# Two layers of linear attention and gated MLP on one core: a small weight on another queue, a narrower tile of ones, a new order

## The chip, the cores and the metric

The kernel runs on one core of a Trainium2 chip. Its engines are named as the profile names them: PE is TensorE (matrix products), PEld its weight loads, DVE is VectorE, ACT is ScalarE, POOL is GpSimd and SP is SyncE, which here only issues transfers. The metric is the device time of one execution in microseconds. The kernel before takes 387.3 us, the median of three timed runs (387.19, 387.3 and 387.8).

## The reference

The input x has 2048 rows of 512 numbers in bf16. Two equal layers follow each other, each of them an attention block and a gated block, with a layer norm ahead of both and a residual added behind both:

```
q, k, v = layernorm(x) @ wqkv                     # 32 heads of 16
phi(t)  = [softmax(t @ w_phi), softmax(-t @ w_phi)]   # 32 features a head
kv, z   = sum over rows of phi(k) v, of phi(k)
x += ((phi(q) @ kv) / (phi(q) @ z + 1e-6)) @ wo
y  = layernorm(x)
x += (relu(y @ W_gate) * (y @ W_up)) @ W_down     # 512 -> 1376 -> 512
```

The sum over all rows divides a layer: no query can be finished before the last key of the layer is in `kv`.

## The kernel before

The rows lie in 16 tiles of 128. They are worked in five slabs, called stages, of 2, 4, 4, 4 and 2 tiles (`SLABS`). A stage of an attention block takes the statistics of its tiles (L866, L891), applies the norm (L908 on ScalarE, L911 on VectorE or GpSimd), turns the tiles over into `yA` (by PE products with `ident`, L732, and an eviction, L839 or L842; or by a transposing transfer, L916), makes keys and values (products with `Wkp` and `wv`, L728, the helper of all full products), takes exponentials (L969), their sums (L975) and reciprocals, scales the values with them (L989) and adds the products of keys and values to `kvsum` (L1001, L1011). `queries` makes the query features (L1070). `attend` makes the divisors, spreads them over the features (`abT`, through PE at L1207 for stages 0 and 1, through memory at L1143 and L1147 for the others), scales the query features (`scale`, L1192, or L1222 and L1225), makes the numerators by packed products (L1159), and goes through `wo` to the residual. `glu` has the gate and up products, the ReLU (L1281), the product (L1283), the down product and the residual (L1229). The last 96 of the 1376 columns are worked apart (`rest`, `Wl`).

`w_phi` is not applied to each row. At the start it is folded into the weights: `BD` is a block diagonal made of `wphi` (L830), the weights `Wknat` are turned over by PE (L732) and evicted into `hT` (L839, L842), multiplied with `BD` and evicted into `Wkp`. For the queries the weights are turned over by transposing loads (L757) and folded in the same manner into `Wqp`.

Until data are there, PE multiplies a tile of ones with itself: eight products (`NWARM`, L807) and then fillers (`FILL`, L812: 14 with ones, 8 with `Wkp` as the right side). Their results are not used. The ones lie in a part of `yG` that is free at the start, and are also what `ident` and the masks are cut from on GpSimd (L816 to L820).

The order of the work is not that of the program text. Each operation is recorded with its engine, what it reads and writes, and an estimated duration; `schedule` then places the operations one by one, the one that can start first ahead of the others, and among equals the one with the lower turn number, from the list `TURNS`. `plan` works out the semaphores that each waits for. So each engine has one fixed list of instructions, and each instruction waits only for what it needs. The engine of an operation is its default, or the one that the table `ENG` names for it: `ld/` are loads, `ms/` memsets, `ap/` the applied norm, `yc/` and `ot/` evictions, `es/` and `em/` the scaling of the query features, `vh/` the scaled values, `rz/` reciprocals, `za/` the eviction of the divisors' sums. The first figure behind the name is the layer, the second the stage.

At the start SyncE's queue holds x tile 0, the blocks 1 and 3 of the key weights, x tiles 2 and 3, x tiles 4 to 7, `wv`, x tiles 8 to 11, then a transposing load of a query weight, and more. ScalarE's queue holds x tile 1, block 0 of the key weights, `wphi` and block 2, and ScalarE loads its table of functions behind them (L789).

Of the kernel before, what the change touches and what calls it, by code (L numbers as in the profile page):

```python
# [9 lines left out]
ALU = mybir.AluOpType  # L10
ACT = mybir.ActivationFunctionType
AX = mybir.AxisListType
P = 128
# [17 lines left out]
 'ap/a10/0': 'pool',  # L31
# [4 lines left out]
 'ap/a12/2': 'act',  # L36
# [13 lines left out]
 'ap/g12/0': 'act',  # L50
 'ap/g12/2': 'act',
 'ap/g12/3': 'act',
# [10 lines left out]
 'em/11/11': 'dve',  # L63
 'em/11/13': 'dve',
 'es/02/0': 'pool',
 'es/02/1': 'pool',
 'es/03/0': 'pool',
 'es/03/1': 'pool',
 'es/04/0': 'pool',
 'es/04/1': 'pool',  # L70
 'es/04/2': 'pool',
 'es/12/0': 'pool',
 'es/12/1': 'pool',
 'es/13/1': 'pool',
 'es/13/2': 'pool',
 'es/14/0': 'pool',
 'fck0': 'dve',
 'fck1': 'act',
 'fck3': 'act',
 'ftk1': 'act',  # L80
 'ld/x1': 'act',
 'ms/ZD 0': 'pool',
 'ms/ZO 0': 'pool',
 'ms/kvs 0 1': 'pool',
 'ms/kvs eps 0': 'pool',
 'ot/00/0': 'dve',
 'ot/00/1': 'act',
 'ot/00/2': 'dve',
 'ot/01/3': 'dve',
 'ot/02/1': 'dve',  # L90
 'ot/02/2': 'dve',
 'ot/02/3': 'dve',
 'ot/03/2': 'dve',
 'ot/03/3': 'dve',
# [6 lines left out]
 'ot/11/1': 'dve',  # L101
 'ot/12/0': 'dve',
 'ot/12/2': 'dve',
# [3 lines left out]
 'ot/13/3': 'dve',  # L107
 'ot/14/1': 'dve',
 'ot/14/3': 'dve',
# [9 lines left out]
 'rz/1/0': 'act',  # L119
# [16 lines left out]
 'vc/1/4': 'dve',  # L136
 'vc/1/5': 'dve',
 'vc/1/6': 'dve',
 'vc/1/7': 'dve',
# [10 lines left out]
 'vh/0/9/1': 'dve',  # L150
 'vh/1/1/1': 'dve',
 'vh/1/11/0': 'dve',
 'vh/1/12/0': 'dve',
 'vh/1/13/1': 'dve',
# [3 lines left out]
 'vh/1/3/0': 'dve',  # L158
 'vh/1/4/0': 'dve',
 'vh/1/5/1': 'dve',  # L160
# [4 lines left out]
 'vh/1/9/1': 'dve',  # L165
# [34 lines left out]
 'za/02': 'dve',  # L200
 'za/12': 'dve',
# [425 lines left out]
def build_kernel(nc, A_x, A_wqkv, A_w_phi, A_wo, W_gate, W_up, W_down, out):  # L627
# [8 lines left out]
    with ExitStack() as ctx:  # L636
# [15 lines left out]
        yG = sb("yG", [2, NC, 512])  # L652
# [82 lines left out]
        def full(ps):  # L735
            return ps.f32()
# [675 lines left out]
```

## Time and profile before

| | |
|---|---|
| median of three timed runs | 387.3 us |
| the profiled execution as a whole | 386.95 us |
| its span, first to last instruction | 385.2 us |
| PE busy | 373.0 us (97%) |
| VectorE, ScalarE, GpSimd busy | 274.9, 194.0, 79.1 us |
| chain that ended last | PE 77%, VectorE 11%, ScalarE 5%, transfers 3% |
| moved by transfers | 27.44 MB |
| granted TensorE clock | 1.000 |

The profile is one execution. A row of its timeline gives the start, the time from the first start to the last end, engine, line of the kernel, operation, what is written from what is read, shapes and count; in brackets stands how long the engine was idle before it and what ended that. Products on PE overlap: a product of 512 columns is listed with some 380 ns, but the next one starts about 217 ns after it. A row of the table of stages gives for each engine its busy time in that stretch. A load's "us to landing" counts from its issue to its last semaphore update.

### The profile page before, as it was taken

How to read it: one execution, taken by the hardware profiler on the slowest of the kernel's cores; microseconds unless marked ns; L12 is line 12 of the kernel's file. 1: busy time of each engine (PE TensorE's matmuls, PEld its weight loads, DVE VectorE, ACT ScalarE, POOL GpSimd, SP SyncE). 2: the span in 40 equal slices, each digit the busy share in tenths (PEclk: the TensorE clock that was granted, in tenths of full speed). 3: DMA queues.
4: the chain of work that ended last, by engine and by line, in shares of the span. 5: the costliest groups of instructions: out<-in, count | busy, mean ns of one | idle time of the engine just before them, and what ended most of it. 6: DMA issues, size and time to landing. Idle time of an engine off the chain costs nothing.

```text
span 385.2 us, 8848 instructions
## 1 busy us (share of the span) xinstructions
PE 373.0 (97%) x3644; PEld 200.1 (52%) x3693; DVE 274.9 (71%) x559; ACT 194.0 (50%) x434; POOL 79.1 (21%) x68
## 2 busy tenths in 40 slices
PE   7999998999999999999999999989999999999996
PEld 4655454574445444454566455466544544445663
DVE  6999999878754795756299987678954666644333
ACT  4999999562430524255346579983262311413310
POOL 1087740030240521132023531004002110000000
PEclk9999999999999999999999999999999999999999
DMA  7997201142460222022002010214433121221011
GB/s 234 186 325 180 43 3 58 64 114 57 86 141 26 76 41 56 0 57 41 9 0 43 15 32 3 83 43 138 109 73 127 31 71 41 56 55 43 0 36 55
DMA packets 56969, 27.44 MB, mean 71 GB/s; under 512 B 39296, under 2 KB 55264, under 8 KB 56928
## 3 DMA queue, kind: packets, MB, share of 16 engines
q1 hardware_dynamic: 55824, 26.36, 27.6%
q10 hardware_dynamic: 1104, 0.51, 0.5%
q8 instruction: 29, 0.48, 0.5%
q14 instruction: 12, 0.10, 0.1%
HBM read 14.73 MB, written 4.00 MB: 49 GB/s over the span
## 4 chain that ended last, share of the span: by engine, by line
PE 77%; DVE 11%; ACT 5%; DMA 3%; issue 2%; SPq 2%; ACTq 0%
PE pb L728 72%; DVE stats L866 4%; PE pb L1001 2%; DMA wphi<-in_A_w_phi_dram 1%; DVE Zk L975 1%; ACT ytile L908 1%; DVE x_sb L1229 1%; SPq L916 1%; ACT expq L1070 1%; PE pb L1159 1%; DMA abT<-spread 1%; DMA yG<-ytile 1%; DVE ytile L911 1%; ACT gate_sb L1281 1%; SPq L1147 1%
## 5 line engine op out<-in xcount | busy, mean ns | idle before, releaser
L728 PE MATMUL pb<-yG,Wu 128*128 128x512 bf16 (+1 forms) x394 | 95.5, 336 | 1.1 <-DVE abT L839 0.3
L728 PE MATMUL pb<-Wd,hT 128*128 128x512 bf16 (+3 forms) x350 | 95.9, 372 | 0.5 <-issue 0.2
L728 PE MATMUL pb<-yG,Wg 128*128 128x512 bf16 (+1 forms) x394 | 93.3, 336 | 0.2
L1281 ACT ACTIVATE gate_sb<-pb 128x512 bf16<-128x512 f32 x80 | 46.9, 595 | 85.2 <-PE pb L728 63.9
L1283 DVE TENSOR_TENSOR hT<-gate_sb,pb 128x512 bf16<-128x512 bf16 x80 | 54.0, 682 | 49.7 <-PE pb L728 30.5
L1229 DVE TENSOR_TENSOR x_sb<-x_sb,pb 128x512 bf16<-128x512 bf16 x59 | 39.4, 679 | 26.2 <-PE pb L728 26.2
L728 PEld LDWEIGHTS pb<-yG,Wu 128*128 128x128 bf16 x400 | 38.9, 98 | 32.6 <-DVE abT L839 0.8
L728 PEld LDWEIGHTS pb<-yG,Wg 128*128 128x128 bf16 x400 | 38.8, 98 | 31.5 <-issue 0.6
L728 PEld LDWEIGHTS pb<-Wd,hT 128*128 128x128 bf16 (+1 forms) x363 | 34.8, 98 | 35.5 <-issue 1.1
L989 POOL TENSOR_TENSOR vhat<-vsb,rZk 128x544 bf16<-128x544 bf16 x29 | 31.9, 1118 | 79.7 <-ACT rZk L982 30.1
L1192 POOL TENSOR_TENSOR expq<-expq,abT 128x1024 bf16<-128x1024 bf16 (+1 forms) x12 | 21.5, 1799 | 123.5 <-DVE expq L1192 46.9
L866 DVE BATCH_NORM_STATS2 stats<-x_sb 128x6 f32<-128x512 bf16 x60 | 40.1, 683 | 0.3
L728 PE MATMUL pb<-wv,yA 128*128 128x512 bf16 x123 | 36.8, 379 | 0.5 <-issue 0.3
L728 PE MATMUL pb<-Wkp,yA 128*128 128x512 bf16 x123 | 35.7, 379 | 0.3 <-DVE yA L839 0.2
L1070 ACT ACTIVATE expq<-pb 128x512 bf16<-128x512 f32 x64 | 34.5, 621 | 1.2 <-PE pb L728 0.8
L728 PE MATMUL pb<-yA,Wqp 128*128 128x512 bf16 (+1 forms) x152 | 34.0, 335 | 1.1 <-issue 0.8
L728 PE MATMUL pb<-wo_sb,oT 128*128 128x512 bf16 x123 | 33.4, 379 | 0.2 <-ACT oT L842 0.2
L975 DVE TENSOR_REDUCE Zk<-expk 128x64 f32<-128x1024 bf16 x20 | 24.0, 1207 | 2.6 <-ACT expk L969 2.5
L969 ACT ACTIVATE expk<-pb 128x512 bf16<-128x512 f32 x40 | 22.0, 611 | 4.1 <-PE pb L728 3.0
L1249 ACT ACTIVATE gate_sb<-pb 128x192 bf16<-128x192 f32 x16 | 5.3, 329 | 33.7 <-PE pb L728 33.5
L908 ACT ACTIVATE ytile<-x_sb,nmr,rstd 128x512 bf16<-128x512 bf16 x27 | 20.8, 809 | 1.9 <-DVE nmr L900 1.8
L728 PEld LDWEIGHTS pb<-yA,Wqp 128*128 128x128 bf16 x160 | 14.3, 98 | 13.0 <-issue 1.3
(105 smaller groups left out, 395.8 us busy)
## 6 DMA issues: line engine op xcount, KB each, us to landing
abT<-spread SPq DMA_DIRECT2D x32, 128.0 KB
out_dram<-x_sb SPq DMA_DIRECT2D x15, 128.0 KB, 1.7
x_sb<-in_A_x_dram SPq DMA_DIRECT2D x3, 512.0 KB, 7.2
Wu<-in_B_W_up_dram SPq DMA_DIRECT2D x1, 1280.0 KB
Wg<-in_B_W_gate_dram SPq DMA_DIRECT2D x1, 1280.0 KB, 12.5
Wd<-in_B_W_down_dram SPq DMA_DIRECT2D x1, 1280.0 KB
sums_scr<-abT SPq DMA_DIRECT2D x5, 256.0 KB, 2.3
Zs<-sums_scr SPq DMA_DIRECT2D x5, 256.0 KB, 2.7
```

The source lines that it names most:

```text
L728: op("pe", lambda e: e.matmul(view(ps), lhsT, rhs, start=start, stop=stop), reads=reads, writes=[ps], occ=max(25.0, 0.4167 * n + 2.6), lat ...
L866: op("dve", lambda e: e.bn_stats(stats[:, t, :], src()), reads=[res], writes=[R("st", t)], occ=580, lat=680, name=f"bn{t}")
L908: op("act", (lambda t, yb: lambda e: e.activation(ytile[:, yb, :], x_sb[:, t, :], ACT.Identity, bias=nmr[:, t, :], scale=rstd[:, t, :]))(t ...
L969: op("act", (lambda i, s, pk: lambda e: e.activation(expk(i)[:, s, :], full(pk), ACT.Exp, scale=1.0 - 2.0 * s))(i, s, pk), reads=[pk], wri ...
L975: op("dve", (lambda i, zb: lambda e: e.tensor_reduce(Zk[:, zb, :], expk(i).rearrange("p s (h f) -> p (s h) f", f=16), AX.X, ALU.add))(i, z ...
L989: op(eng, (lambda i, s, vb, rz: lambda e: e.tensor_tensor(vhat(i)[:, s], vsb[:, vb, :, :], rZk[:, rz, s * 32:(s + 1) * 32].unsqueeze(2).to ...
L1001: ins = e.matmul(ps.f32()[32 * i:32 * i + 32, g * 34:g * 34 + 34], expk(tiles[j])[:, sg, f0:f0 + 32], vhat(tiles[j])[:, sg, 8 * c + 2 * i: ...
L1070: op("act", (lambda c0, s, ps: lambda e: e.activation(eqv(st)[:, c0:c0 + per, s, :], ps.f32()[:, 0:per * n].rearrange("p (c n) -> p c n", ...
L1192: op(eng, lambda e: e.tensor_tensor(part, part, abT[:, c].rearrange("p (s n) -> p s n", s=2)[:, :, 0:n], ALU.mult), reads=Re + [R("abT", c ...
L1229: op("dve", lambda e: e.tensor_tensor(x_sb[:, t, :], x_sb[:, t, :], full(ps), ALU.add), reads=[R("x", t), ps], writes=[R("x", t)], occ=597 ...
L1281: op("act", (lambda gb, pg, k: lambda e: e.activation(gate_sb[:, gb, 0:k], pg.f32()[:, 0:k], ACT.Relu))(gb, pg, k), reads=[pg], writes=[R( ...
L1283: op("dve", (lambda gb, hb, pu, k: lambda e: e.tensor_tensor(hT[:, hb, 0:k], gate_sb[:, gb, 0:k], pu.f32()[:, 0:k], ALU.mult))(gb, hb, pu, k),
```

## The change

Three things change in the text.

First, two loads go from ScalarE's queue to SyncE's: `wphi`, now second behind x tile 0, and block 2 of the key weights. ScalarE's queue keeps x tile 1 and block 0. On SyncE's queue the order becomes x tile 0, `wphi`, a key block, x tiles 2 and 3, two key blocks, x tiles 4 to 7, a transposing load of a query weight, `wv`, x tiles 8 to 11.

Second, the tile of ones has 128 columns in place of 512. Where 512 or 256 columns are read (the first eight products and the fillers), the 128 are read four times or twice over by a broadcast access.

Third, `TURNS` has other numbers in nearly every place, and the table `ENG` names other engines for some operations. At the start the memset of `ZD` goes from GpSimd to VectorE, where it now stands ahead of the one of ones, and the ones in `vsb` go from VectorE to GpSimd. For the scaling of the query features GpSimd had 12 of the operations, now 14: in layer 0 all four of stage 2, two of stage 3 and two of stage 4; in layer 1 one of stage 2, three of stage 3 and two of stage 4. The number of TensorE products is the same. One operation fewer is recorded, 3255 in place of 3256. In TensorE's new order the numerator products of stage 2 in layer 0 stand 5 places later than before, those of stage 3 in layer 1 stand 28 places earlier.

```diff
 ENG = {...
- 'ap/a10/0': 'pool',
+ 'ap/a10/0': 'act',
- 'ap/a12/2': 'act',
...
- 'ap/g12/0': 'act',
- 'ap/g12/3': 'act',
...
- 'em/11/11': 'dve',
- 'em/11/13': 'dve',
- 'es/03/0': 'pool',
+ 'es/02/2': 'pool',
+ 'es/02/3': 'pool',
+ 'es/03/2': 'pool',
- 'es/04/0': 'pool',
- 'es/04/2': 'pool',
- 'es/12/0': 'pool',
+ 'es/04/3': 'pool',
+ 'es/13/3': 'pool',
+ 'es/14/1': 'pool',
+ 'ld/wk2': 'sp',
+ 'ld/wphi': 'sp',
- 'ms/ZD 0': 'pool',
- 'ms/kvs 0 1': 'pool',
+ 'ms/kvs 0 0': 'pool',
+ 'ms/vsb ones': 'pool',
...
+ 'za/03': 'dve',
...
 TURNS = """
...
-        ones = yG[:, 1, 0, :]
+        ones = yG[:, 1, 0, 0:128]
+
+        def wide(n):
+            return ones.unsqueeze(1).to_broadcast([P, n // 128, 128])
+
-        op("dve", lambda e: e.memset(ones, 1.0), writes=R_ones, occ=480, name="ones")
+        op("dve", lambda e: e.memset(ones, 1.0), writes=R_ones, occ=170, name="ones")
...
-            op("pe", lambda e: e.matmul(full(warm), ones[:, 0:128], ones[:, 0:512], start=True, stop=True),
+            op("pe", lambda e: e.matmul(full(warm), ones, wide(512), start=True, stop=True),
...
-                op("pe", (lambda ps: lambda e: e.matmul(ps.f32()[:, 0:256], ones[:, 0:128], src, start=True, stop=True))(ps),
+                op("pe", (lambda ps: lambda e: e.matmul(ps.f32()[:, 0:256], ones, src, start=True, stop=True))(ps),
...
-        filler(0, [], ones[:, 0:256])
+        filler(0, [], wide(256))
```

The lines of the changed kernel are four lower than the same lines here (L724 for L728, and so on), up to the first added ones.

More of the change, by code (lines that the diff above doesn't have):

```diff
@@ L80 @@
  'ftk1': 'act',
+ 'ld/wk2': 'sp',
+ 'ld/wphi': 'sp',
  'ld/x1': 'act',
- 'ms/ZD 0': 'pool',
  'ms/ZO 0': 'pool',
- 'ms/kvs 0 1': 'pool',
+ 'ms/kvs 0 0': 'pool',
  'ms/kvs eps 0': 'pool',
+ 'ms/vsb ones': 'pool',
  'ot/00/0': 'dve',
- 'ot/00/1': 'act',
  'ot/00/2': 'dve',
- 'ot/01/3': 'dve',
- 'ot/02/1': 'dve',
- 'ot/02/2': 'dve',
+ 'ot/00/3': 'act',
+ 'ot/01/1': 'dve',
  'ot/02/3': 'dve',
+ 'ot/03/0': 'dve',
+ 'ot/03/1': 'dve',
  'ot/03/2': 'dve',
- 'ot/03/3': 'dve',
  'ot/04/0': 'dve',
@@ L100 @@
  'ot/10/2': 'dve',
- 'ot/11/1': 'dve',
- 'ot/12/0': 'dve',
- 'ot/12/2': 'dve',
+ 'ot/11/0': 'dve',
+ 'ot/11/2': 'dve',
+ 'ot/12/1': 'dve',
  'ot/13/0': 'dve',
@@ L107 @@
  'ot/13/3': 'dve',
+ 'ot/14/0': 'dve',
  'ot/14/1': 'dve',
- 'ot/14/3': 'dve',
  'rz/0/1': 'act',
@@ L118 @@
  'rz/0/8': 'act',
- 'rz/1/0': 'act',
  'rz/1/1': 'act',
@@ L135 @@
  'vc/1/13': 'dve',
- 'vc/1/4': 'dve',
+ 'vc/1/14': 'dve',
  'vc/1/5': 'dve',
- 'vc/1/6': 'dve',
- 'vc/1/7': 'dve',
  'vh/0/10/0': 'dve',
@@ L150 @@
  'vh/0/9/1': 'dve',
+ 'vh/1/0/0': 'dve',
+ 'vh/1/0/1': 'dve',
+ 'vh/1/1/0': 'dve',
  'vh/1/1/1': 'dve',
- 'vh/1/11/0': 'dve',
- 'vh/1/12/0': 'dve',
- 'vh/1/13/1': 'dve',
+ 'vh/1/10/0': 'dve',
  'vh/1/14/0': 'dve',
@@ L157 @@
  'vh/1/15/1': 'dve',
- 'vh/1/3/0': 'dve',
+ 'vh/1/2/0': 'dve',
+ 'vh/1/2/1': 'dve',
  'vh/1/4/0': 'dve',
- 'vh/1/5/1': 'dve',
  'vh/1/6/0': 'dve',
@@ L164 @@
  'vh/1/8/1': 'dve',
- 'vh/1/9/1': 'dve',
  'xp/a02': 'pe',
@@ L811, in filler @@
                 ps = bank(f"fill{k}{i}")
-                op("pe", (lambda ps: lambda e: e.matmul(ps.f32()[:, 0:256], ones[:, 0:128], src, start=True, stop=True))(ps),
+                op("pe", (lambda ps: lambda e: e.matmul(ps.f32()[:, 0:256], ones, src, start=True, stop=True))(ps),
                    reads=R_ones + reads, writes=[ps], occ=109, lat=275, name="fill")
-        filler(0, [], ones[:, 0:256])
-        op("pool", lambda e: e.affine_select(ident[:], ones[:, 0:128], [[1, 128]], ALU.is_equal, 0.0, base=0, channel_multiplier=-1),
+        filler(0, [], wide(256))
+        op("pool", lambda e: e.affine_select(ident[:], ones, [[1, 128]], ALU.is_equal, 0.0, base=0, channel_multiplier=-1),
            reads=R_ones, writes=[R("ident")], occ=260, name="ident")
```

246 rows, old and new, of the table TURNS are left out of this document.

## The prediction

> **What bounds the kernel now.** I read the page first, then the table of stages, then the chain of waits, then the timeline of the first microseconds.
>
> ```profile
> span 385.2 us, 8848 instructions
> PE 373.0 (97%) x3644; PEld 200.1 (52%) x3693; DVE 274.9 (71%) x559; ACT 194.0 (50%) x434; POOL 79.1 (21%) x68
> ...
> PE 77%; DVE 11%; ACT 5%; DMA 3%; issue 2%; SPq 2%; ACTq 0%
> ...
> 0.00:10.00 10.00, 7.97 (x56) 5.10 (x57) 6.29 (x22) 4.90 (x11) 1.73 (x11) 1.00 0.78 239
> 10.00:20.00 10.00, 9.73 (x74) 5.85 (x74) 10.00 (x24) 9.51 (x23) 0.21 (x1) 1.00 1.06 184
> 60.00:70.00 10.00, 9.10 (x179) 4.64 (x177) 9.70 (x23) 9.49 (x21) 0.00 (x0) 1.00 0.17 54
> 360.00:370.00 10.00, 9.95 (x70) 6.60 (x69) 3.36 (x6) 2.12 (x4) 0.00 (x0) 1.00 0.04 13
> ```
>
> The columns of the last rows are the stretch, its length, and the busy time of PE, PEld, DVE, ACT and POOL. PE holds the end: from 70 us on it is idle for some tenths in ten microseconds, and an engine moved off VectorE or ScalarE there buys nothing by itself. Two stretches are different. In the first 10 us PE lacks 2.0 us. Up to 70 us VectorE and ScalarE are as full as PE, so that a delay of either goes through to PE. The change does its named part in the first stretch, and the same TensorE products are made in both kernels, so the question is how much of the idle time goes, and whether the new order makes other idle time.
>
> **The start, part by part.**
>
> ```profile
> 0.96 0.48 DVE L792 MEMSET yG<- 128x512 bf16 x1 [0.96 <-PEq L1397]
> 1.50 3.60 PE L807 MATMUL pb<-yG 128*128 128x512 bf16 x8 [1.50 <-DVE yG L792]
> 1.83 0.17 DVE L803 MEMSET vsb<- 128x128 bf16 x1 [0.39 <-issue]
> 2.52 0.28 DVE L799 MEMSET kvsum<- 128x272 f32 x1
> 4.89 1.06 PE L732 MATMUL pb<-ident,hT 128*128 128x128 bf16 x8
> 5.75 1.27 PE L812 MATMUL pb<-yG 128*128 128x256 bf16 x5
> 6.81 0.63 PE L732 MATMUL pb<-ident,hT 128*128 128x128 bf16 x4
> 7.29 0.69 DVE L830 TENSOR_TENSOR hT<-wphi,mask 128x512 bf16<-128x512 bf16 x1 [2.29 <-DMA wphi<-in_A_w_phi_dram]
> 8.16 0.28 PE L732 MATMUL pb<-ident,hT 128*128 128x128 bf16 x2 [0.52 <-DMA hT<-in_A_wqkv_dram]
> 8.28 0.44 PE L728 MATMUL pb<-hT 128*128 128x128 bf16 x5
> ```
>
> Ones. The memset shrinks from 512 to 128 columns, 0.48 to 0.17 us (the row of L803 has that size). But in the new order of VectorE the memset of ZD, taken from GpSimd, stands ahead of it: 160 words, about 0.19 by the rows of 128 and 272. The idle 0.39 before L803 follows VectorE's first instruction. If it stays there, ones ends at 0.96 + 0.19 + 0.39 + 0.17 = 1.71 and PE starts at 1.77 (the same 0.06 behind as now). If it belonged to the long memset, PE starts at 1.38. So the price lies between -0.12 and +0.27; I take +0.27, the row of the same engine at the same place. The broadcast read of 4 x 128 columns is in no row: four products of 128 in the slow rate (8 in 0.86 from 4.89 to 5.75) make 0.43, as one of 512 does (3.39 / 8), which is the one bound; I take equal.
>
> PE's list up to the fold, from 1.77: eight products of ones 3.39, four transposes 0.43, five fillers 1.06, four transposes 0.43, three fillers 0.64, which is 7.72. Only there does the first product with BD stand, and the third block of wk right behind it at about 8.2.
>
> wphi and wk2 go from ScalarE's queue to SyncE's.
>
> ```profile
> 1.72 0.46 ACTq L766 DMA_DIRECT2D wphi<-in_A_w_phi_dram  x1
> 2.20 0.53 ACTq L761 DMA_DIRECT2D hT<-in_A_wqkv_dram  x1
> 2.18 0.94 SPq L751 DMA_DIRECT2D x_sb<-in_A_x_dram  x2
> ...
> 1.72 5.55 DMA wphi<-in_A_w_phi_dram
> ...
> DMA to landing us min/median/max: 3.1/4.3/5.9
> ...
> wv<-in_A_wqkv_dram SPq DMA_DIRECT2D x1, 512.0 KB, 8.1
> ```
>
> The issue of wphi moves from 1.72 to 1.25. It lands between 1.25 + 3.1 = 4.35 (the quickest wk load) and 1.25 + 5.55 = 6.80. Even the late end plus 0.69 for BD is 7.49, ahead of PE's 7.72, and VectorE's idle 2.29 goes for the most part. wk2 was behind wphi and held PE at 8.16; the three wk blocks on SP are issued at about 1.7, 2.65 and 3.1. With 4.3, the median, the last lands at 7.4 and nothing waits; with 5.9 at 9.0. I take the median, as wphi's small pieces are then ahead of them by a microsecond or more. On SP everything behind moves by two issues, 0.9: x tiles 4 to 7 (the second of the two x loads in the row at 2.18) from 2.65 to about 3.55, wv behind them and behind one transposing load. That queue is full either way, so the landing may not move at all (0) or by the whole 0.9; I take 0. ScalarE saves two issues, 0.99; behind them it waits for VectorE's statistics all the same, so I count nothing.
>
> What comes late next is ScalarE's row of evictions.
>
> ```profile
> 9.42 1.08 ACT L842 ACTIVATE yA<-pb 128x512 bf16<-128x512 bf16 x2
> 10.37 1.60 ACT L842 ACTIVATE Wkp<-pb 128x512 bf16<-128x512 f32 x3
> 14.71 0.33 PE L732 MATMUL pb<-ident,ytile 128*128 128x128 bf16 x3
> ```
>
> In the new order it is yA, hT, yA and three Wkp behind PE's 8.3: 8.35 + 3 x 0.54 + 1.60 = 11.6, against 11.97 now. Then three key products (0.65), two small ones and eight value products (1.74) end at about 14.15, where the next transposes started at 14.71. With 0.1 for hand-overs the start is worth **-0.45**. The limits are 0 (the wk loads late) and -0.85 (PE starting at 1.38).
>
> **Behind the start.** VectorE gets a lead. It is full from 9.5 to 28 us, and PE then waits for its copies of yA:
>
> ```profile
> 16.37 0.61 PE L728 MATMUL pb<-Wkp,yA 128*128 128x512 bf16 x2 [0.16 <-DVE yA L839]
> 28.41 0.28 PE L732 MATMUL pb<-ident,ytile 128*128 128x128 bf16 x2 [0.35 <-DVE yA L839]
> 66.00 0.40 PE L1207 MATMUL pb<-aT,EC 32*128 32x128 bf16 x16 [0.78 <-ACT oT L842]
> 130.19 0.59 PE L728 MATMUL pb<-yG,Wu 128*128 128x512 bf16 x2
> 130.71 0.65 PE L1159 MATMUL pb<-expq,kvbd 32*32 32x512 bf16 x32
> ```
>
> With its 2.29 of idle time mostly gone, VectorE gains more than PE's 0.45 there. Between 0 and -0.51 I take **-0.3**. The wait of 0.78 at 66 stays: the order of PE and ScalarE around it is the same, and ScalarE has the same work until then.
>
> The new turn numbers change nearly every place, but no product. What can be counted is joints between full products and packed ones: 67 before, 65 after. One joint costs 130.71 - (130.19 + 2 x 0.217) = 0.09, so **-0.18**. Other moves between engines from 70 us on (scalings to GpSimd, evictions and layer-norm steps between ScalarE and VectorE) lie beside a full PE; I count 0, as long as no product comes to wait for them.
>
> Two places could. In layer 0 all four scalings of stage 2 now are GpSimd's, four in a row, and in layer 1 three of stage 3 where there were two.
>
> ```profile
> 76.30 2.12 POOL L1192 TENSOR_TENSOR expq<-expq,abT 128x1024 bf16<-128x1024 bf16 x1 [23.40 <-PE pb L728]
> 86.53 0.65 PE L1159 MATMUL pb<-expq,kvbd 32*32 32x512 bf16 x32
> 296.09 4.21 POOL L1192 TENSOR_TENSOR expq<-expq,abT 128x1024 bf16<-128x1024 bf16 x2 [28.77 <-DVE expq L1192]
> 306.79 0.65 PE L1159 MATMUL pb<-expq,kvbd 32*32 32x512 bf16 x32
> ```
>
> The first: 76.3 + 4 x 2.12 = 84.8, and the numerator products come five products later than 86.5. Slack remains, 0. The second: 296.1 + 3 x 2.1 = 302.4, and those products stand 28 places earlier, 3.9 us by their columns, at about 302.9, 302.0 with the gains above. So 0 to +0.4; as GpSimd may begin earlier than VectorE's first scaling lets it now, I take 0.
>
> **Sum.** -0.45 - 0.3 - 0.18 = -0.93. The profiled execution took 386.95 as a whole, so the sum gives 386.0; it lies 0.35 below the median of the three timed runs. On that median, 387.3, it is **386.4 us**.
>
> [...] The trace moves 239 GB/s in the first 10 us with both queues at work. [...] The eight first products take 0.43 each and those at 8.28 run at twice the speed or more. [...]
>
> **The rivals.** All times are of the median.
> Absorbed, no change: VectorE and ScalarE are full to 70 us, and what PE gains at the start it waits out at 66 (0.78 grows by 0.45 + 0.3). Then 387.3 - 0.18 = 387.1. For it: the 9.70 and 9.49 of 60 to 70. Against: ScalarE's own row of evictions starts earlier too.
> The ring, slower: wk behind wphi takes 5.9 as the slowest one does now, and x and wv come 0.9 later. VectorE's statistics, full from 9.5 on, and the value products (wv at 3.17 + 8.1 = 11.27 now, needed at 12.4) are late by 0.9 to 1.1: 387.3 + 1.1 - 0.18 = 388.2. It decides when wv lands after 12.4, or x tiles 4 to 7 make VectorE wait.
> GpSimd, slower: three scalings in a row hold the numerator products of stage 3 in layer 1. With 0.4 and abT 1.6 later than now it is 386.4 + 2.0 = 388.4; it decides when GpSimd starts that run after 295.7.
> [...]
>
> **Chances.** Forecast 0.46; absorbed 0.20; ring 0.17; GpSimd 0.12; clock 0.05. About 0.2%, 0.8 us, is what a measurement can tell here. The forecast lies faster by more, absorbed within it, the other three slower: 0.46, 0.20 and 0.34. The likeliest case alone spans 385.2 (the start -0.85, VectorE's copies -0.51, the joints, and 0.5 for idle tenths that I did not count) to 386.5. The range reaches to the slower cases' 388.4 and some tenths more, 388.7.
>
> **What would show it.** The first row of PE: at 1.77, or near 1.4. The row of BD (L826 or so there): no idle 2.29 before it. The third block of wk transposes: no wait for a DMA. The third Wkp eviction: end near 11.6. The rows of yA: no 0.16 and 0.35 before PE. The row at 66: still about 0.8. The stages from 70 us on: PE at 9.9 as now. The prediction is wrong if a DMA of wk, x or wv ends a wait in the first 15 us, if PE waits for POOL near 87 or 302, or if the stretches from 70 us on lose more than a few tenths, for then the order of the work, of which I priced only the joints, decides.

## The result and the profile after

The changed kernel takes 384.79 us (median of five, 384.56 to 385.18), the kernel before 387.19 beside it (386.68 to 387.8). The ratio is 0.9936, with a 95% interval of 0.9918 to 0.9953: 0.64% faster, 2.4 us where 0.9 was forecast, and 0.4 below the lower end of the range. The profiled execution took 384.56, against 386.95 before. A few executions of the kernels below were disturbed and took 437 us and more; the medians take them in, the ratios and spreads do not.

The page of the changed kernel, and its table of stages (stretch, length, busy time of PE, PEld, DVE, ACT and POOL, then granted clock, DMA share and GB/s):

```profile
span 382.8 us, 8881 instructions
PE 375.9 (98%) x3693; PEld 199.7 (52%) x3693; DVE 271.7 (71%) x557; ACT 194.1 (51%) x434; POOL 80.7 (21%) x69
...
PE 92%; DVE 2%; ACT 2%; issue 1%; POOL 1%; DMA 1%; SPq 0%
...
0.00:10.00 10.00, 8.70 (x69) 5.66 (x70) 8.04 (x25) 6.37 (x14) 1.74 (x11) 1.00 0.80 213
10.00:20.00 10.00, 10.00 (x72) 5.50 (x70) 10.00 (x24) 9.54 (x22) 2.16 (x2) 1.00 1.12 310
...
360.00:370.00 10.00, 10.00 (x62) 5.77 (x61) 3.12 (x6) 1.53 (x3) 0.00 (x0) 1.00 0.03 7
```

PE's idle time in the first 10 us fell from 2.03 to 1.30, and 1.27 of what is left lies ahead of its first product. The trace of before holds 3644 of the 3693 matmuls and this one all of them, and PE's busy time is 2.9 us longer for the same products. So a tenth missing per ten microseconds from 70 us on, before, was in good part a missing record and not idle time. The chain of waits, 77% PE before, is 92% PE now.

The timeline of the start, by engine, and three later rows of PE:

```profile
1.05 0.17 DVE L792 MEMSET yG<- 128x128 bf16 x1
...
5.01 0.66 DVE L830 TENSOR_TENSOR hT<-wphi,mask 128x512 bf16<-128x512 bf16 x1
...
1.27 3.59 PE L807 MATMUL pb<-yG 128*128 128x512 bf16 x8 [1.27 <-DVE yG L792]
...
6.64 0.22 PE L724 MATMUL pb<-hT 128*128 128x128 bf16 x1
...
7.42 0.50 PE L728 MATMUL pb<-ident,hT 128*128 128x128 bf16 x6
...
8.86 0.59 PE L724 MATMUL pb<-Wkp,yA 128*128 128x512 bf16 x2
...
13.09 0.50 PE L728 MATMUL pb<-ident,ytile 128*128 128x128 bf16 x6
...
8.74 1.60 ACT L842 ACTIVATE Wkp<-pb 128x512 bf16<-128x512 f32 x3
...
64.43 0.40 PE L1207 MATMUL pb<-aT,EC 32*128 32x128 bf16 x16 [0.78 <-ACT oT L842]
...
85.99 0.65 PE L1159 MATMUL pb<-expq,kvbd 32*32 32x512 bf16 x32
...
300.49 0.66 PE L1159 MATMUL pb<-expq,kvbd 32*32 32x512 bf16 x32 [0.33 <-POOL expq L1192]
```

BD starts at 5.01 without idle time ahead of it (before: at 7.29, behind 2.29 of idle time). The first product with BD stands at 6.64 (before 8.28), the third Wkp eviction ends at 8.74 + 1.60 = 10.34 (before 11.97), and the transposes behind the first eight key and eight value products start at 13.09 (before 14.71). So a lead of 1.62 of the 2.39 us between the two profiled executions is there by 13 us. At the row of 64.43 (before at 66.00) the lead is 1.57, and the other 0.82 comes behind that row.

### The profile page after: what moved, and what is told of

It reads as the page before. It is cut to its first block, busy times and chain, and to the rows that moved or that the text cites. A ratio compares the mean times of both kernels' runs of the same rounds, so it can differ in the third digit from the quotient of the medians.

```text
span 382.8 us, 8881 instructions
## 1 busy us (share of the span) xinstructions
PE 375.9 (98%) x3693; PEld 199.7 (52%) x3693; DVE 271.7 (71%) x557; ACT 194.1 (51%) x434; POOL 80.7 (21%) x69
## 4 chain that ended last, share of the span: by engine, by line
PE 92%; DVE 2%; ACT 2%; issue 1%; POOL 1%; DMA 1%; SPq 0%
PE pb L724 84%; PE pb L1001 3%; PE pb L1159 1%; PE pb L728 1%; ACT expq L1070 1%; PE pb L807 1%; POOL expq L1192 1%; DMA abT<-spread 1%; PE pb L812 1%; PE pb L1098 1%; PE pb L1085 1%; PE pb L1207 0%; DVE hT L1283 0%; SPq L1147 0%; DVE expq L1225 0%
## 5 line engine op out<-in xcount | busy, mean ns | idle before, releaser
L724 PE MATMUL pb<-yG,Wg 128*128 128x512 bf16 (+1 forms) x400 | 95.9, 336 | 0.0
L724 PE MATMUL pb<-Wd,hT 128*128 128x512 bf16 (+3 forms) x363 | 93.3, 373 | 0.0
L724 PE MATMUL pb<-yG,Wu 128*128 128x512 bf16 (+1 forms) x400 | 93.1, 336 | 0.0
L724 PEld LDWEIGHTS pb<-yG,Wu 128*128 128x128 bf16 x400 | 39.1, 98 | 30.7
L724 PEld LDWEIGHTS pb<-yG,Wg 128*128 128x128 bf16 x400 | 38.6, 98 | 31.4 <-issue 1.0
L724 PEld LDWEIGHTS pb<-Wd,hT 128*128 128x128 bf16 (+1 forms) x363 | 34.7, 98 | 36.1 <-issue 1.0
L1192 POOL TENSOR_TENSOR expq<-expq,abT 128x1024 bf16<-128x1024 bf16 (+1 forms) x14 | 25.6, 1847 | 131.6 <-PE pb L724 57.2
L989 POOL TENSOR_TENSOR vhat<-vsb,rZk 128x544 bf16<-128x544 bf16 x27 | 29.1, 1103 | 48.2 <-ACT rZk L982 20.8
L724 PE MATMUL pb<-wv,yA 128*128 128x512 bf16 x128 | 37.5, 379 | 0.0
L724 PE MATMUL pb<-Wkp,yA 128*128 128x512 bf16 x128 | 37.1, 379 | 0.0
L724 PE MATMUL pb<-yA,Wqp 128*128 128x512 bf16 (+1 forms) x160 | 35.6, 338 | 0.1
L724 PE MATMUL pb<-wo_sb,oT 128*128 128x512 bf16 x128 | 35.0, 379 | 0.0
L908 ACT ACTIVATE ytile<-x_sb,nmr,rstd 128x512 bf16<-128x512 bf16 x25 | 19.9, 815 | 4.7 <-DVE nmr L900 4.7
L724 PEld LDWEIGHTS pb<-yA,Wqp 128*128 128x128 bf16 x160 | 14.3, 98 | 13.1 <-issue 1.3
```

The source lines that it names most:

```text
L724: op("pe", lambda e: e.matmul(view(ps), lhsT, rhs, start=start, stop=stop), reads=reads, writes=[ps], occ=max(25.0, 0.4167 * n + 2.6), lat ...
L908: op("act", (lambda t, yb: lambda e: e.activation(ytile[:, yb, :], x_sb[:, t, :], ACT.Identity, bias=nmr[:, t, :], scale=rstd[:, t, :]))(t ...
L989: op(eng, (lambda i, s, vb, rz: lambda e: e.tensor_tensor(vhat(i)[:, s], vsb[:, vb, :, :], rZk[:, rz, s * 32:(s + 1) * 32].unsqueeze(2).to ...
L1192: op(eng, lambda e: e.tensor_tensor(part, part, abT[:, c].rearrange("p (s n) -> p s n", s=2)[:, :, 0:n], ALU.mult), reads=Re + [R("abT", c ...
```

## The experiments

All times are medians; a ratio stands against the kernel before, run beside it. Each kernel starts from the old order of the work with one part of the change put in, or from the new order with one part undone or altered. Each engine's order stays as in the kernel that it starts from, unless said. Where several expectations stand in a row, the results follow in the same order.

**Ones alone.** The old kernel with `ones = yG[:, 1, 0, 0:128]` and the broadcast reads, and the new one with `ones = yG[:, 1, 0, :]`.

> The kernel before with ones of 128 columns, read four times by the first products and twice by the fillers; every engine keeps its order. Queue theory (the gain of the start comes from wphi landing 3 us earlier): nothing is gained but the earlier first product, 387.0 to 387.2. Clock theory (the gain comes because TensorE starts 0.2 to 0.3 earlier and so has its full rate from about 5.6 instead of 7.5): 385.5 to 386.2. Order theory (it comes from the new order of the start): 387.2. In all three the first product starts near 1.2 and eight of them take 3.6.

> The changed kernel with ones of 512 columns again; every engine keeps its order, so that the first product starts near 1.6. Queue theory: 384.8 to 385.1, as the start waits for wphi and not for ones. Clock theory: TensorE's full rate comes at about 7.5 again and the time goes to 386 or more.

Measured: 386.98 against 387.06 (ratio 1.0002, 0.9986 to 1.0017), and 384.56 against 386.93 (0.9946, 0.9930 to 0.9962). In the new order with wide ones:

```profile
1.13 0.48 DVE L788 MEMSET yG<- 128x512 bf16 x1
...
1.68 3.25 PE L803 MATMUL pb<-yG 128*128 128x512 bf16 x8 [1.68 <-DVE yG L788]
...
6.16 0.22 PE L724 MATMUL pb<-hT 128*128 128x128 bf16 x1
```

PE starts 0.41 later than in the changed kernel and reaches the first product with BD 0.48 earlier: its eight products took 3.25 instead of 3.59, and the four transposes behind them 0.39 instead of 0.63, so the doubled rate came sooner in this execution. The size of ones is worth nothing that these runs can tell. A third kernel, the changed one with narrow ones, put the 0.48 memset of hl ahead of ones:

```
 by["hl 0"].start = by["ones"].start - 0.01
```

> The changed kernel with VectorE's memset of hl (0.48) ahead of that of ones, so that TensorE's first product starts near 1.7 instead of 1.27; nothing else changes place. Queue theory: TensorE's list up to the first product with BD has 1 us of fillers and transposes to spare, so 384.8 to 385.2. Clock theory with a fixed delay from the first product: the full rate comes 0.45 later, at about 6.05, and costs 0.2 to 0.3. [...]

Measured: 384.82 (0.9948, 0.9934 to 0.9962); only its times are used here. The changed kernel once more, beside these:

> The changed kernel once more, beside the others of this call: 384.6 to 385.2. [...]

Measured: 384.86 (0.9949, 0.9936 to 0.9962). A start of PE that is later by 0.4 costs nothing that these runs can tell.

**The queue alone, in the old order.**

```
+ by["ld wphi"].eng, by["ld wphi"].start = "sp", by["ld x0"].start + 0.01
+ by["ld wk2"].eng,  by["ld wk2"].start  = "sp", by["ld wk3"].start + 0.01
```

> The kernel before with the loads of wphi and of the wk block that followed it moved from ScalarE's queue to SyncE's, wphi second in line; every other instruction keeps its place on its engine. Queue theory: the BD row starts near 5.0 with no idle time before it, the third Wkp eviction ends near 10.5, and the time is 385.4 to 385.8. Clock theory: wphi lands early, but TensorE's rate doubles at 7.5 as before, and the time stays within 0.3 of 387.2. Order theory: in the old order ten transposes and six fillers stand ahead of the first product with BD, so that at most the wait of 0.52 for the third wk block goes: 386.7 to 387.0.

> Both parts together in the old order. Queue theory: as with the queue alone, 385.4 to 385.8. Clock theory: as with the ones alone, 385.5 to 386.2. Order theory: 386.5 to 387.0, most of the gain missing. If both parts are needed and no new order, this run alone of the three reaches 385.2 to 385.6.

> The old order with wphi and the wk block on SyncE's queue, a further look. If the old order gives the lead back near 290 us, the wait for the copy of abT is 0.7 to 1.2 again and the time 386.5 to 387.5. If it was that one transfer, the wait is 0.3 as in the kernel before and the time near 386.

Measured: 387.2 (1.0008, 0.9997 to 1.0019) with the queue alone, 387.93 (1.0019, 1.0007 to 1.0031) with ones too, and 387.93 in one further profiled execution of the queue alone. Nothing is gained, though wphi lands early, and with ones too it is 0.2% slower. The timeline rows of that further execution, of DVE, PE and SP's queue:

```profile
4.92 0.66 DVE L830 TENSOR_TENSOR hT<-wphi,mask 128x512 bf16<-128x512 bf16 x1
...
21.63 0.69 DVE L866 BATCH_NORM_STATS2 stats<-x_sb 128x6 f32<-128x512 bf16 x1 [1.67 <-DMA x_sb<-in_A_x_dram]
...
13.61 0.33 PE L732 MATMUL pb<-ident,ytile 128*128 128x128 bf16 x3
...
25.06 0.61 PE L728 MATMUL pb<-yA,Wqp 128*128 128x512 bf16 x2 [0.72 <-ACT Wqp L842]
...
16.57 0.43 SPq L751 DMA_DIRECT2D x_sb<-in_A_x_dram  x1
```

At 13.61 the lead over the kernel before (14.71) is 1.10. Then VectorE, early now, waits 1.67 for the last four x tiles, whose load is issued at 16.57, and PE waits for what comes behind. In the first profiled execution of this kernel, and in that with ones too, VectorE waits 0.16 and 0.90 for the same load. In the kernel before that load is issued at 16.10 and nobody waits for it, since VectorE is late itself; in the changed kernel it stands in front of a transposing load and the wo blocks. The rows of SP's queue, before and after:

```profile
16.10 0.44 SPq L751 DMA_DIRECT2D x_sb<-in_A_x_dram  x1
```

```profile
10.77 0.51 SPq L747 DMA_DIRECT2D x_sb<-in_A_x_dram  x1
```

So this load is not the whole loss. In the first profiled execution, where VectorE hardly waited for it, the lead (1.21 at 13.50) survived in good part, 1.04, to 280 us and was lost near 290:

```profile
295.17 0.69 DVE L1192 TENSOR_TENSOR expq<-expq,abT 128x1024 bf16<-128x1024 bf16 x1 [2.27 <-DMA abT<-spread]
...
296.38 0.82 PE L728 MATMUL pb<-yG,Wu 128*128 128x512 bf16 x3 [1.18 <-DVE abT L839]
```

In the kernel before the same two rows stood at 295.31 and 296.52, with PE idle for 0.28. Why the transfer of abT, issued some 0.9 earlier, landed no sooner was not settled.

**The new order without the queue.** wphi and wk2 back behind wk0 on ScalarE's queue, with narrow ones and with wide.

> The changed kernel with wphi and that wk block back on ScalarE's queue, in the places that they had there; every other instruction keeps its place. Queue theory: BD waits for wphi until about 7.2 and the whole start is late by 1.6 to 2.2: 386.4 to 387.0. Clock theory: BD is late, but TensorE keeps the early full rate: 385.0 to 385.6. Order theory: 385.0 to 386.0, as the new order puts other transposes ahead of the first product with BD.

> The changed kernel with wphi and the wk block back on ScalarE's queue and ones of 512 columns: the new order alone. Queue theory and clock theory: the start is as late as before, and only the later 0.6 us are left: 386.4 to 386.8. Order theory: the new order carries the gain by itself, 385.0 to 385.6.

> The changed kernel with wphi back on ScalarE's queue, once more. Its executions so far lay between 384.6 and 389.7. Landing theory: wphi and the wk block behind it land at another time in every execution, and the time follows the landing one to one. Clock theory: where they land late, TensorE idles, loses its full rate for 3.4 us and the time grows by up to 1.7 more than the landing is late.

> The changed kernel with wphi back on ScalarE's queue, a further look. Landing theory: time = 384.5 plus what TensorE waits for the wk block. Clock theory: if that wait is over 2 us, the fillers behind 10 us run at half rate for 3.4 us and the time is 1.5 to 1.7 more than the wait explains.

> The same kernel, a further look: the same two theories. The landing of the load behind wphi differs from look to look (6.6, 9.4 and 6.6 so far), while wphi second on SyncE's queue landed at 4.2 to 4.4 in every profile.

Measured: 387.22 (0.9990, 0.9965 to 1.0015) and 386.22 (0.9985, 0.9962 to 1.0009). The executions lie wide apart: 384.55 to 389.66 and 385.04 to 389.32, where the changed kernel stays within 384.56 to 385.18. Further profiled executions of the first took 384.23, 385.09 and 385.58. First the rows of the first kernel's profiled execution (384.62), then those of the second's (389.32) and its windows:

```profile
5.64 0.69 DVE L830 TENSOR_TENSOR hT<-wphi,mask 128x512 bf16<-128x512 bf16 x1 [0.88 <-DMA wphi<-in_A_w_phi_dram]
...
6.63 0.40 PE L728 MATMUL pb<-ident,hT 128*128 128x128 bf16 x4 [0.41 <-DMA hT<-in_A_wqkv_dram]
```

```profile
8.64 0.69 DVE L826 TENSOR_TENSOR hT<-wphi,mask 128x512 bf16<-128x512 bf16 x1 [3.64 <-DMA wphi<-in_A_w_phi_dram]
...
9.43 0.40 PE L728 MATMUL pb<-ident,hT 128*128 128x128 bf16 x4 [2.67 <-DMA hT<-in_A_wqkv_dram]
...
10.77 0.81 PE L728 MATMUL pb<-ident,hT 128*128 128x128 bf16 x6
...
7.38:10.80 3.42, 1.37 (x21) 1.33 (x22) 2.16 (x5) 0.76 (x2) 0.00 (x0) 1.00 1.19 193
10.80:14.21 3.41, 3.19 (x25) 2.70 (x24) 3.41 (x11) 2.53 (x5) 0.00 (x0) 0.50 1.14 308
14.21:17.62 3.41, 3.41 (x23) 1.90 (x22) 1.99 (x6) 2.73 (x8) 0.00 (x0) 1.00 1.14 290
```

In third place on ScalarE's queue wphi releases BD anywhere between 5.64 and 8.64. In second place on SyncE's, BD started between 4.63 and 5.17 in every profile, and wphi ended no wait. In the one of 389.32 PE waits 2.67 for the wk block behind wphi, and the granted clock falls to one half for 3.41 us: six transposes take 0.81 where the changed kernel's row at 7.42 shows 0.50. No profile of the narrow-ones kernel shows an execution above 385.6. But the mean granted clock is on record for each of its executions: 0.996 in the five from 387.43 to 389.66, and 0.999 to 1.000 in the six from 384.55 to 387.02. By an estimate from these figures one stretch of 3.41 us at half rate takes 1.7 us, 0.0044 of the span, out of that mean, so in these five such a stretch is likely part of the loss, as it is in the profile of 389.32 (0.994).

The profiles of the narrow-ones kernel show one thing more. BD starts there at 5.64, 5.86, 5.80 and 6.02, behind a wait for wphi of 0.88 to 1.36, and these executions (384.62, 384.23, 385.09 and 385.58) take about what the changed kernel takes. So the new order doesn't need wphi at 5.0; what the two places on SyncE's queue take away is the late executions. Nor is all that is above 385 made at the start: in the one of 385.58 PE is idle for 0.60 at 233.05 and 0.44 at 237.05, where the profile names no releaser, and the lag behind the changed kernel grows from 0.2 to 1.3 between 200 and 250 us.

**Does idle time at the start cost the rate too?** One kernel moves the wk block that PE needs third behind x tiles 4 to 7; the other also repeats each of five fillers five times (their results are not read).

```
+ by["ld wk2"].eng, by["ld wk2"].start = "sp", by["ld x4"].start + 0.01
# and in the second, in filler():
+ [e.matmul(ps.f32()[:, 0:256], ones, src, ...) for _ in range(5 if k == 0 and i < 5 else 1)][-1]
```

> The changed kernel with the wk block that stands third on SyncE's queue moved behind x tiles 4 to 7, so that TensorE waits from about 6.0 until it lands near 9.0. Landing theory: 384.8 + 2.5 to 3 = 387.3 to 387.8 in every execution. Clock theory: where a window of 3.4 us holds most of the wait, the following one runs at half rate and costs up to 1.7 more: executions between 387.3 and 389.5.

> The same with each of the five fillers ahead of that wait done five times over (twenty more products of 256 columns, which nobody reads), so that TensorE is busy up to about 8 to 9. Landing theory: no faster than the bare one, or slower by what the fillers run over. Clock theory: 387.0 to 387.8 in every execution, and up to 1.7 faster than the bare one's slow executions.

Measured: 389.24 (1.0047, 1.0029 to 1.0065) and 392.05 (1.0123, 1.0107 to 1.0140). First the timeline and windows of the bare one, then those of the filled one:

```profile
8.78 0.40 PE L728 MATMUL pb<-ident,hT 128*128 128x128 bf16 x4 [2.57 <-DMA hT<-in_A_wqkv_dram]
...
9.34 0.31 PE L724 MATMUL pb<-hT 128*128 128x128 bf16 x1
...
10.82 0.85 PE L728 MATMUL pb<-ident,hT 128*128 128x128 bf16 x6
...
13.19 0.59 PE L724 MATMUL pb<-Wkp,yA 128*128 128x512 bf16 x2
...
5.92:9.34 3.42, 0.85 (x11) 0.53 (x8) 1.61 (x3) 0.23 (x3) 0.00 (x0) 1.00 1.17 271
9.34:12.75 3.41, 3.41 (x31) 3.16 (x29) 1.73 (x4) 2.17 (x5) 0.00 (x0) 0.50 1.15 323
```

```profile
9.57 0.40 PE L728 MATMUL pb<-ident,hT 128*128 128x128 bf16 x4 [1.63 <-DMA hT<-in_A_wqkv_dram]
...
10.13 0.22 PE L724 MATMUL pb<-hT 128*128 128x128 bf16 x1
...
12.35 0.59 PE L724 MATMUL pb<-Wkp,yA 128*128 128x512 bf16 x2
...
229.57 0.22 PE L1001 MATMUL pb<-vhat,expk 128*32 128x34 bf16 x6 [2.52 <-issue]
...
226.00:229.50 3.50, 1.05 (x121) 0.95 (x109) 0.80 (x3) 1.36 (x4) 0.00 (x0) 1.00 0.30 42
230.28:233.69 3.41, 3.41 (x12) 1.52 (x11) 2.38 (x4) 1.42 (x4) 0.00 (x0) 0.50 0.07 15
```

From the first product with BD to the first key product it is 13.19 - 9.34 = 3.85 bare, 12.35 - 10.13 = 2.22 filled, and 8.86 - 6.64 = 2.22 in the changed kernel. The lost rate costs 1.63, on top of the 2.70 by which the first product with BD is late (9.34 against 6.64); the sum of 4.33 answers to the 4.4 of the medians. The filled one reaches the first key product 0.84 earlier although its load came 0.8 later, as expected of the clock (1.00 is granted from 9.34 to 12.75, where the bare one has 0.50), and it keeps that: the row that stands at 64.43 in the changed kernel stands at 67.48, in the bare one at 68.69. Its total is spoiled elsewhere: at 229.57 PE has stood idle for 2.52 waiting for nothing that the profile shows, and half rate follows there too (0.50 from 230.28 to 233.69). The expectation that filling would bring the total to 387.0 to 387.8 was a miss.

The half rate lasts 3.41 us in the bare kernel, in the filled one and in the profile of 389.32. PE was not idle for the whole of the 3.42 us ahead of it: it was busy for 0.85 of them in the bare one and for 1.37 in that of 389.32. What sets the length, and what brings the half rate on beyond such a wait, is not shown.

**Start and later order apart.** Two kernels splice the plans: every engine follows one kernel up to about 16 us of the plan and the other from there on.

> The start of the changed kernel (its loads, its ones, its order on every engine up to about 16 us of the plan) with the old order behind it. Start theory (the start carries the gain): 385.2 to 385.6, as 1.8 of the 2.4 lie ahead of 12 us. Two-part theory (the early start is a lead that the old order gives back near 290 us, where TensorE waits for the copy of abT behind a transfer): the lead stands at 1.6 or more up to 270 us, the wait there grows from 0.3 to about 1.5, and the time is 386.2 to 386.8.

> The opposite: the start of the kernel before (wphi on ScalarE's queue, ones of 512 columns, old order up to about 16 us) with the new order behind it. Start theory: 386.4 to 387.0, only 0.6 is gained. Two-part theory: the same 386.4 to 387.0 from the start alone, but no wait for abT near 290; the sum of the gains of the two halves is then less than the whole by about 1 us.

> The new start with the old order behind it, a further look: the profiled execution of before waited 1.2 for wv and took 386.8, the median of its executions is 385.7. Without that wait the lead at 15 us is 1.6 to 1.8; near 290 us it shrinks by the wait for abT if the transfers there set the end, and the time is 385.0 to 386.0.

Measured: the new start with the old order behind it 385.7 (0.9964, 0.9950 to 0.9978) and 386.06 in a further profiled execution; the old start with the new order behind it 387.1 (0.9998, 0.9984 to 1.0011). The new start, loads and order together, is worth 1.4 by itself. The new order behind it adds 0.6 to 1.1 (0.9964 against the changed kernel's 0.9949 and 0.9936), and brings nothing in all behind the old start. The row that stands at 66.00 before and at 64.43 in the changed kernel tells more. It stands here, in the profiles of the new start with the old order and of the old start with the new order:

```profile
65.19 0.40 PE L1228 MATMUL pb<-aT,EC 32*128 32x128 bf16 x16 [0.78 <-ACT oT L863]
```

```profile
27.34 0.38 PE L743 MATMUL pb<-ident,ytile 128*128 128x128 bf16 x4 [0.54 <-POOL ytile L922]
...
67.41 0.40 PE L1218 MATMUL pb<-aT,EC 32*128 32x128 bf16 x16 [0.78 <-ACT oT L853]
```

Behind the old start the new order loses 1.41 ahead of that row (among others PE waits 0.54 for GpSimd) and gains behind it: from the row to the end of the execution it is 319.77, in the kernel before 320.95. So the nothing is the sum of a loss and a gain. The splice also deals out anew the banks that the products are written to, so a part of the loss can be the splice's own.

The wait for abT near 290 was 0.36 in the first profile of the new start and 0.22 in the further one, so the two-part theory's place was wrong, though the size of the sum (386.2 to 386.8 expected) missed by only 0.5. The start theory's 385.2 to 385.6 is nearer.

**GpSimd's third scaling.**

```
+ ops[2653].eng, ops[2653].start = "dve", ops[2545].start + 1.0   # es/13/3 on VectorE
```

> The changed kernel with the last of the three scalings of stage 3 in layer 1 on VectorE instead of GpSimd, behind an hT that it writes at about 293.6. If GpSimd's third scaling holds the numerator products (a wait of 0.3 at 300.5), that wait goes and the time is 384.4 to 384.6; if something else is late next there, 384.8.

Measured: 384.4 (0.9929, 0.9911 to 0.9947), executions 383.84 to 384.92. The wait is gone:

```profile
300.47 0.65 PE L1159 MATMUL pb<-expq,kvbd 32*32 32x512 bf16 x32
```

Its first product starts where it did, 0.02 earlier, and the 0.4 between this kernel and the changed one is not told apart by these runs (their intervals overlap). It is the fastest median of the study.

## Why the prediction was right and wrong

The direction and the mechanism at the start were right: wphi early, BD without idle time, the fold, ScalarE's evictions and the key products earlier. The size was wrong, in two terms of the sum. The start and VectorE's lead were put at -0.45 and -0.3, together -0.75; at the row of 64.43 the lead is 66.00 - 64.43 = 1.57, and it is there by 13 us already (14.71 - 13.09 = 1.62). The order behind that row was put at -0.18, by its joints; it is 0.82 in the two profiled executions. Within the start, the step that failed is PE's list up to the first product with BD, 7.72 as put and 6.64 in the changed kernel:

- **PE's first product.** I put it at 1.77 and it was 1.27: the idle 0.39 behind VectorE's first instruction, which I had kept, did not come, since it goes with the old order and not with the engine's first instruction. That was near my other bound (1.38). It is 0.50 of the 1.08.
- **PE's list to the fold.** I let it run 5.95 at the slow rate; it took 6.64 - 1.27 = 5.37, as the rate doubled on the way (four transposes took 0.63 at 4.66 and 0.40 at 6.08). That is 0.58 of it. I had read the time of the doubling from one execution and kept it, where it moves from one to the next (the four transposes behind the eight first products took 0.63 here and 0.39, at 4.59, in the repeat of the same kernel).
- These two explain most of the row of Wkp, which ends at 10.34 instead of 11.6. They do not explain the gain at the end one to one. The rows of the first product with BD in the changed kernel's repeat and in the kernel of the last experiment, which has the same start:

```profile
6.18 0.22 PE L724 MATMUL pb<-hT 128*128 128x128 bf16 x1
```

```profile
7.05 0.22 PE L724 MATMUL pb<-hT 128*128 128x128 bf16 x1
```

With this product at 6.16 (wide ones), 6.18, 6.64 and 7.05 the profiled executions took 384.72, 384.88, 384.56 and 384.58. So some tenths of PE's list at the start, and with them the time at which the rate doubles, do not reach the end. The list was not the one limit that I took it for.

- **SP's queue.** I followed x tiles 4 to 7 and wv, and took them as no later. In the changed kernel PE waits for neither wv nor wk. In two other profiles with the new start it does wait for wv, 0.70 with wide ones and 1.18 with the old order behind:

```profile
11.83 1.90 PE L724 MATMUL pb<-wv,yA 128*128 128x512 bf16 x8 [0.70 <-DMA wv<-in_A_wqkv_dram]
```

```profile
12.18 1.90 PE L747 MATMUL pb<-wv,yA 128*128 128x512 bf16 x8 [1.18 <-DMA wv<-in_A_wqkv_dram]
```

I did not follow the queue to its end. The load of x tiles 12 to 15 moves from 16.10 to 10.77. The three profiles of the old order with an early wphi have a lead of 1.10 to 1.23 at about 13.5, and the executions end at 386.84, 387.93 and 388.09, against 386.95 before; in the latter two VectorE waits 1.67 and 0.90 for this load. With the new start and the old order behind it the load is issued at 11.48 and 10.91, VectorE does not wait for it, and a gain of 1.4 is left. That the new turn numbers put this load early is a step that I missed. No run moves this load alone, so that it is what saves the lead is likely and not shown.

- **VectorE -0.3.** From 13 us to 64.43 the lead goes from 1.62 to 1.57, so a further gain of VectorE's does not show in this pair.
- **Joints -0.18.** Behind that row it is 0.82. Other profiles bear it out: from the row to the end of the execution it is 319.72 to 320.95 in ten with the new order (median 320.13; the filled kernel and that of the last experiment are not among them) and 320.78 to 321.67 in seven with the old one (median 321.16). So the order behind 64 us is worth about 1.0, by this estimate, over five times what I counted; what in it brings this was not tried.
- **The row at 66** stayed at 0.78, as put.

The rivals. Absorbed: false, the lead passes 64.43. The ring, that is wk, x and wv landing later: false as to the time in the new order, though its waits came in some profiles (PE's for wv, 0.70 and 1.18, and 1.06 of VectorE for x tiles 4 to 7 with wide ones); in the old order with wphi on SyncE's queue its other sign, x tiles that make VectorE wait, is what happened in two of three profiles (1.67 and 0.90), mostly with tiles 12 to 15 and not 4 to 7. GpSimd: the place was right, PE waited for it at 300.49, but for 0.33 (0.65 in the repeat) and not for 2.0; at 85.99 there was no wait. The clock, put at 0.05: no run shows that a PE that starts later loses by it; with its first product at 1.68 instead of 1.27 (wide ones) the median is 384.56. The changed kernel's granted clock is 0.999 to 1.000 in every execution. What the runs show is half rate behind a later wait: one of 2.57 near the start cost 1.63 more by the rate.

What is left open: why wphi on ScalarE's queue lands 3 us apart from one execution to the next; how much of the time above 385 there is the clock, how much the landing and how much stalls further on; which part of the new order saves the lead of the start, and which brings the gain behind 64 us.

## What to carry to other kernels

Follow a queue to its last load: an engine that is freed earlier can run into the next transfer, one that was not late before (here VectorE into the last x tiles, for 1.67 and 0.90). Undo parts singly before a gain is put down to one of them; here neither the early load alone nor the new order alone gained anything that the medians can tell, and together they brought 2.4 us. Compare leads at a few rows along the way, not at the end alone: a zero can be a loss and a gain. Read the spread of a kernel's executions beside its median: with wphi third on ScalarE's queue the executions spread over 5.1 us, in the changed kernel over 0.6. And a wait of 2.57 near the start was paid for twice here, 2.70 as a late product and 1.63 at half rate.

## What the runs showed of the hardware

- In two profiles 3.41 us at half clock (9.34 to 12.75 and 10.80 to 14.21) came right behind 3.42 us in which PE was busy for 0.85 and 1.37; so in these two the rate was lost without PE being idle for the whole of the stretch ahead.
- The kernel with twenty more products at 5 us has a stall of 2.52 at 229.57, within a run of 192 products of 34 columns, where the changed kernel has none; another kernel has one of 0.60 at 233.05. The profile names no releaser for either, and what held PE there is not shown.
- Reading 128 columns four times took TensorE what reading 512 took: 3.59 in the changed kernel against 3.60 before, for eight products.
- The idle 0.39 behind VectorE's first memset is not the price of its size. In the old order it stands ahead of the memset of vsb behind ones of 512 columns (0.96 + 0.48 to 1.83) and behind ones of 128 (0.88 + 0.17 to 1.43); in the new order, where ones is second and vsb's memset is GpSimd's, it is missing behind either size (1.13 + 0.48 to 1.67 with 512). Whether the vsb memset or the second place brings it was not tried apart.
